# Per-head decays loaded as eight numbers and spread on the chip; zeros of the states on GpSimd

## The chip, the cores and the metric

The kernel runs on one core of a Trainium2 chip. The metric is the device time of one execution in microseconds (us). The time before is the median of three runs; a profiled execution of its own gives the trace that all readings are from. Engines: PE is TensorE, PEld its weight loads, DVE is VectorE, ACT is ScalarE, POOL is GpSimd, SP is SyncE, which issues most of the transfers.

## The reference, cut to what matters

```python
B, H, S, D = 4, 8, 768, 64            # block = 64
rel = pos[:, None] - pos[None, :]
Dmask = where(rel >= 0, lam[:, None, None] ** rel, 0.0)
lam_pow = lam[:, None, None] ** (pos[None, :, None] + 1)
for b in range(S // 64):
    intra = ((qb @ kb.T) * Dmask) @ vb
    inter = (qb * lam_pow) @ kv_state
    out[:, :, sl] = intra + inter
    kv_state = lam ** 64 * kv_state + (kb * lam ** (63 - pos)).T @ vb
x = out, heads side by side            # 3072 x 512
h = x @ w_in                           # 512 x 2048
g = maximum(h, 0) + alpha * minimum(h, 0)
return g @ w_out                       # 2048 x 512
```

`lam` holds one decay for each of the eight heads; all decay factors of the attention are powers of it.

## The kernel before

The attention is computed in blocks of 128 positions, two of them (256 rows) at a time. A unit is one batch entry, one half of the heads (four of them) and 256 rows; `units` lists 24 of them, four to a step `c`. For each unit the raw k, q and v are loaded (`load`, on SP's queue), cast to fp16 (`cast`, k16, q16, v16), k is also multiplied by its decay (`key_decayed`, line 256), q and k are transposed (`transposes`: eight PE transposes at line 284 and a copy of the result `tp` to `qkT`, or a transfer that transposes), and the transposed q is multiplied by its decay (`decayed`, line 299). `cluster(old, new)` then computes the scores `s` of the new unit (line 341), its state update `acc` (line 368), the masked scores `sm` on DVE (line 379, scores times `dmask`), and the output of the old unit (lines 324 and 353), which is copied to `xT`. States are kept in `R`, and in `RD` as blocks with zeros off the diagonal; the zeros are written once at the start (line 120).

`up(c, f)` is the first matrix product of the second part with its activation (lines 431, 439, 448), `down` the second (line 461), `down_last` that of the last step (line 484).

The order of instructions on each engine is the order in which the program issues them: the schedule is manual, each engine's queue is in order, and waits come from the data. The opening is written out by hand (lines 523 to 727), as a list of calls; after it `weave` interleaves attention and matrix products. Transfers go on SP's queue (k, q, v, output), on GpSimd's (the weights, `load_win` and `load_wout`) and two small ones at the start on ScalarE's (lam and alpha). `fill(n)` issues n products of `ident` with itself whose result nobody reads.

All decay tables come from `loglam`, the logarithm of lam on all 128 partitions. Before, `lam` is loaded to all partitions by one transfer whose source has a step of zero over the partitions (line 61), clamped on DVE (`lamc`, line 156), and its logarithm is taken on ScalarE (line 158). An earlier activation of a column of ones (`warm`, line 124) also uses Ln. `loglam` feeds `llp` (lines 192 and 193), the eight logarithmic mask steps of `mask_logs` on DVE (line 173), `key_decay` (line 189, behind a load of the table for Exp), `query_decay` (line 205), `state_decay` (line 197) and `decay_mask` (line 183). The head of the opening is this:

```python
mask_logs(3); mask_logs(0); key_decay()
load(0, 0, "k", 0); cast(0, "k16", "A"); query_decay(2, 1)
...
cast(0, "q16", "G"); decay_mask(3); fill(29)
transposes(0, "V", False); decayed(0, "V"); cast(2, "k16", "A")
...
cast(1, "q16", "G"); cast(0, "v16", "G"); state_decay(); decay_mask(1)
fill(30); cluster(None, 0)
```

"A", "V" and "G" name the engine: ScalarE, VectorE, GpSimd.

Of the kernel before, what the change touches and what calls it, by code (L numbers as in the profile page):

```python
# [11 lines left out]
def kernel(  # L12
# [16 lines left out]
    nc = tc.nc  # L29
    ctx.enter_context(tc.manual_schedule())  # L30
    fp32 = mybir.dt.float32
    fp16 = mybir.dt.float16
    int32 = mybir.dt.int32
    AF = mybir.ActivationFunctionType
    ALU = mybir.AluOpType

    B, H, S, D = q.shape
# [7 lines left out]
    NF = DFF // 128  # L45
    CH = 2 * W

    const = ctx.enter_context(tc.tile_pool(name="const", bufs=1))
# [8 lines left out]
    ps = ctx.enter_context(tc.tile_pool(name="ps", bufs=1, space=bass.MemoryType.PSUM))  # L57
    h_ps_pool = ctx.enter_context(tc.tile_pool(name="hps", bufs=2, space=bass.MemoryType.PSUM))

    lam_sb = const.tile([128, H], fp32, name="lam_sb")  # L60
    nc.scalar.dma_start(
        out=lam_sb,
        in_=bass.AP(tensor=lam.tensor, offset=lam.offset, ap=[[0, 128]] + [list(p) for p in lam.ap]),
    )


    R = {
        (b, hh, n): const.tile([128, 2, D], fp16, name=f"R{b}_{hh}_{n}")
# [4 lines left out]
    RD = {  # L73
        (b, hh): const.tile([128, 2, 2, 2, D], fp16, name=f"RD{b}_{hh}")
        for b in range(B)
        for hh in range(2)
    }
# [35 lines left out]
        x = 4 * (which == "out") + i  # L113
        nc.sync.dma_start(out=gates16[:, x : x + 1], in_=w)

    alpha_sb = const.tile([NF, 128], fp32, name="alpha_sb")
    nc.scalar.dma_start(out=alpha_sb, in_=moe_alpha.rearrange("(t p) -> t p", p=128))

    for t in RD.values():
        nc.vector.memset(t, 0.0)  # L120
    one = const.tile([128, 1], fp32, name="one")
    nc.vector.memset(one, 1.0)
    warm = const.tile([128, 1], fp32, name="warm")
    nc.scalar.activation(warm, one, AF.Ln)
    ident = const.tile([128, 128], fp16, name="ident")
    make_identity(nc, ident)
    ident32 = const.tile([NF, NF], fp32, name="ident32")
    nc.vector.tensor_copy(out=ident32, in_=ident[0:NF, 0:NF])

    rel_i = const.tile([128, 3, 64], int32, name="rel_i")
    for half in range(2):
# [7 lines left out]
        out=drop, in0=rel_i, scalar1=0.0, scalar2=-1e30, op0=ALU.is_lt, op1=ALU.mult  # L141
    )
    rev_i = const.tile([128, 2], int32, name="rev_i")
    for half in range(2):
        nc.gpsimd.iota(
            rev_i[ds(half * 64, 64)], pattern=[[-1, 2]], base=L - 1, channel_multiplier=-2
        )
    rev_f = const.tile([128, 2], fp32, name="rev_f")
    nc.vector.tensor_copy(out=rev_f, in_=rev_i)
    pos_i = const.tile([128, 2, 2, 64], int32, name="pos_i")  # L150
    nc.gpsimd.iota(pos_i, pattern=[[1, 2], [0, 2], [2, 64]], base=1, channel_multiplier=0)
    pos_f = const.tile([128, W], fp32, name="pos_f")
    nc.vector.tensor_copy(out=pos_f, in_=pos_i.rearrange("p e h j -> p (e h j)"))

    lamc = const.tile([128, H], fp32, name="lamc")
    nc.vector.tensor_scalar(out=lamc, in0=lam_sb, scalar1=1e-18, scalar2=None, op0=ALU.max)
    loglam = const.tile([128, H], fp32, name="loglam")
    nc.scalar.activation(loglam, lamc, AF.Ln)
    llv = loglam.rearrange("p (n two) -> p two n", two=2)

    dmask = const.tile([128, 2, NHP, 3, 64], fp32, name="dmask")
# [45 lines left out]
    def slopes():  # L207
# [2 lines left out]
        nc.vector.tensor_scalar(  # L210
            out=oma, in0=at[:, 0:NF], scalar1=-1.0, scalar2=1.0, op0=ALU.mult, op1=ALU.add
        )

    def fill(n):

        t = ps.tile([128, CH], fp32, tag="op", name="op_fill")
        for _ in range(n):
            nc.tensor.matmul(t[:, 0:128], lhsT=ident, rhs=ident, start=True, stop=True)  # L218

    T = {}  # L220
    XT = {}
# [17 lines left out]
    def cast(n, name, eng):  # L239
        t = T.setdefault(n, {})  # L240
        if name == "v16":
            t[name] = half_pool.tile([128, 2, 4, D], fp16, tag=name, name=name)
            copy_on(eng, t[name], raw_of(n)[name])
            return
        if "qk16" not in t:
            t["qk16"] = half_pool.tile([128, 2, 2, 4, D], fp16, tag="qk16", name="qk16")
        copy_on(eng, t["qk16"][:, int(name == "k16")], raw_of(n)[name])
# [21 lines left out]
    def transposes(n, eng, decay=True):  # L269

        t = T[n]
        qkT = qkt_pool.tile([128, 2, 2, 2, L], fp16, tag="qkT", name="qkT")
        if eng == "D":
            nc.sync.dma_start(
                out=qkT.rearrange("p x e h j -> p (x e h) j"),
                in_=t["qk16"].rearrange("p x e h d -> p (x e h d)"),
                transpose=True,
            )
        else:
            tp = ps.tile([128, 2, 2, 2, L], fp16, tag="tk", name="tp")  # L280
            for x in (1, 0):
                for e in range(2):
                    for hp in range(2):
                        nc.tensor.transpose(  # L284
                            tp[:, x, e, hp, :],
                            t["qk16"][:, x, e, ds(2 * hp, 2)].rearrange("p l d -> p (l d)"),
                            ident,
                        )
            copy_on(eng, qkT, tp)
        t["qkT"] = qkT  # L290
        if decay:
            decayed(n)
# [250 lines left out]
    cast(0, "q16", "G")  # L543
    decay_mask(3)
    fill(29)
    transposes(0, "V", False)
    decayed(0, "V")
# [6 lines left out]
    state_decay()  # L554
    decay_mask(1)
    fill(30)
    cluster(None, 0)
    load(0, 1, "k", 1)
# [9 lines left out]
    query_decay(3, 1)  # L568
    key_decayed(2, "V")
    cast(2, "q16", "G")  # L570
    fill(22)
    cluster(0, 1, "A")
    load(1, 0, "k", None)
    load(1, 0, "q", None)
# [6 lines left out]
    cast(2, "v16", "A")  # L581
    decayed(1, "V")
    cast(3, "q16", "A")
    fill(16)
    cluster(1, 2, "A")
    decayed(2, "G")
    transposes(3, "A", False)
    fill(21)
    cluster(2, 3, "A")
    up(0, 3, 0, "h")  # L590
    decayed(3, "G")
# [178 lines left out]
```

## Time and profile before

| | |
|---|---|
| median of 3 runs | 222.5 us (222.31 to 222.65) |
| profiled execution | 222.39 us, span 220.6 us |
| busy, share of the span | PE 94%, DVE 60%, ACT 52%, PEld 51%, POOL 42% |
| chain that ended last, by engine | PE 82%, DMA 5%, ACT 3%, DVE 2%, issue 2% |
| lam's transfer | 4.0 KB, 3.8 us from issue to landing |
| the first twelve loads on SP's queue | 256.0 KB each, the last issued at 9.90 us |

Times in the profile count from the start of the span. In a line of the timeline the first number is the start and the second the time from the first start to the last end, then engine, line, operation, result and operands, shape and count; in brackets stands the idle time in front of it and what ended it. In the chain of waits each piece has its start, its length and what it was. In the table by stage each row gives the busy time of each engine in that stretch, with the number of instructions, the granted PE clock, the share of the DMA engines and the rate of the transfers.

### The profile page before, as it was taken

What the parts mean: (1) busy time and instruction counts of PE and PEld (TensorE: products, weight loads), DVE (VectorE), ACT (ScalarE), POOL (GpSimd) and SP (SyncE); (2) the same over time, 40 slices, a digit from 0 to 9 for tenths busy, and PEclk for the clock granted to TensorE, in tenths of its full rate; (3) what the DMA queues carried; (4) which work ended last, traced back from release to release, by engine and by line L of the source; (5) the groups of instructions that cost most, each with busy time, mean ns of one, the idle gap of its engine ahead of it and who ended that gap; (6) DMA issues with size and microseconds to landing.
All of it is one profiled execution on the core that took longest, in us unless ns stands there. A gap on an engine that the chain in (4) does not pass through costs nothing.

```text
span 220.6 us, 5380 instructions
## 1 busy us (share of the span) xinstructions
PE 208.4 (94%) x2165; PEld 111.7 (51%) x2165; DVE 131.8 (60%) x255; ACT 114.6 (52%) x217; POOL 93.0 (42%) x165
## 2 busy tenths in 40 slices
PE   5697899999996999999999999999999999999994
PEld 5686544564454544545544554544555444444453
DVE  6986488877597974777645656546655544444000
ACT  4897587555464575355465444465544434444121
POOL 3783065533486583676353774433774100000000
PEclk9799999999999999999999999999999999999998
DMA  4999999995999999779448689343231011100212
GB/s 123 296 252 209 273 280 208 199 221 147 151 327 208 299 260 209 153 197 239 117 74 216 149 188 250 83 101 89 51 95 52 0 48 52 48 32 16 95 51 95
DMA packets 62463, 33.92 MB, mean 154 GB/s; under 512 B 18262, under 2 KB 59494, under 8 KB 62438
## 3 DMA queue, kind: packets, MB, share of 16 engines
q1 hardware_dynamic: 58038, 29.37, 53.8%
q0 software_dynamic: 4224, 4.19, 11.5%
q8 instruction: 17, 0.28, 0.6%
q14 instruction: 8, 0.07, 0.1%
q10 hardware_dynamic: 176, 0.01, 0.0%
HBM read 27.28 MB, written 6.29 MB: 152 GB/s over the span
## 4 chain that ended last, share of the span: by engine, by line
PE 82%; DMA 5%; ACT 3%; issue 2%; DVE 2%; SPq 2%; POOL 2%; ACTq 0%; DVEq 0%
PE h_ps L431 35%; PE o_ps L461 30%; PE o_ps L484 6%; PE s L341 4%; PE acc L324 3%; PE acc L353 3%; DMA kraw<-in_k_dram 2%; DMA qkT<-qk 2%; SPq L88 2%; PE acc L368 1%; DVE sm L379 1%; DVE R L403 1%; POOL kdec L256 1%; PE tp L284 1%; ACT RD L399 1%
## 5 line engine op out<-in xcount | busy, mean ns | idle before, releaser
L448 DVE SCALAR_TENSOR_TENSOR g<-m,oma,h_ps 128x512 f16<-128x512 f32 (+1 forms) x98 | 71.2, 736 | 61.3 <-ACT m L439 59.6
L431 PE MATMUL h_ps<-xT,w_in_sb 128*128 128x512 f16 (+1 forms) x392 | 94.7, 375 | 0.1
L439 ACT ACTIVATE m<-h_ps 128x512 f32<-128x512 f32 (+1 forms) x98 | 57.3, 588 | 66.0 <-PE h_ps L431 65.3
L461 PE MATMUL o_ps<-w_out_sb,g 128*128 128x512 f16 x320 | 81.1, 379 | 0.0
L431 PEld LDWEIGHTS <-w_in_sb 128*128 128x128 f16 x392 | 37.6, 98 | 43.5 <-issue 0.2
L461 PEld LDWEIGHTS <-g 128*128 128x128 f16 x320 | 29.8, 98 | 34.0 <-issue 0.2
L379 DVE TENSOR_TENSOR sm<-s,dmask 128x512 f16<-128x512 f32 x48 | 30.8, 683 | 5.7 <-PE s L341 5.1
L299 POOL TENSOR_TENSOR qdT<-qkT,qdecay 128x512 f16<-128x512 f16 (+1 forms) x21 | 22.2, 1058 | 27.0 <-DMA qkT<-qk 11.8
L417 POOL COPY RD<-R 64x128 f16<-64x128 f16 x64 | 18.5, 289 | 34.8 <-DVE R L403 33.1
L474 ACT ACTIVATE o_sb<-o_ps 128x512 f32<-128x512 f32 (+1 forms) x25 | 14.5, 579 | 15.5 <-PE o_ps L484 11.1
L256 POOL TENSOR_TENSOR kdec<-kraw,kdecay 128x512 f16<-128x512 f32 x20 | 21.2, 1061 | 2.2 <-DMA kraw<-in_k_dram 2.1
L226 ACT ACTIVATE xT<-acc 128x512 f16<-128x512 f32 x22 | 13.1, 597 | 14.8 <-PE acc L368 9.8
L403 DVE SCALAR_TENSOR_TENSOR R<-R,rdecay,acc 128x64 f16<-128x64 f16 x64 | 14.2, 274 | 1.8 <-ACT R L400 1.8
L230 POOL CAST v<-vraw 128x512 f16<-128x512 f32 x20 | 13.0, 657 | 2.7 <-DMA vraw<-in_v_dram 2.7
L484 PE MATMUL o_ps<-w_out_sb,g 128*128 128x512 f16 (+1 forms) x80 | 14.0, 336 | 0.0
L218 PE MATMUL op_fill<-ident 128*128 128x128 f16 x140 | 12.0, 258 | 1.4 <-POOL ident masks.py:199 1.4
L341 PE MATMUL s<-qkT 64*64 64x128 f16 x384 | 10.1, 223 | 1.8 <-DMA qkT<-qk 1.7
L324 PE MATMUL acc<-qdT,RD 128*128 128x128 f16 x80 | 8.9, 219 | 3.0 <-DVE R L403 1.8
L218 PEld LDWEIGHTS <-ident 128*128 128x128 f16 x140 | 10.9, 119 | 1.5 <-POOL ident masks.py:199 1.4
L484 PEld LDWEIGHTS <-g 128*128 128x128 f16 x80 | 7.8, 98 | 6.2
L226 ACT ACTIVATE qk<-qraw 128x512 f16<-128x512 f32 x16 | 10.0, 623 | 1.3 <-DMA qraw<-in_q_dram 1.3
L324 PEld LDWEIGHTS <-RD 128*128 128x128 f16 x80 | 5.8, 97 | 9.0 <-ACT qkT L226 1.6
(54 smaller groups left out, 111.4 us busy)
## 6 DMA issues: line engine op xcount, KB each, us to landing
out_dram<-o_sb SPq DMA_DIRECT2D x23, 256.0 KB, 2.5
kraw<-in_k_dram SPq DMA_DIRECT2D x10, 512.0 KB, 5.5
qraw<-in_q_dram SPq DMA_DIRECT2D x10, 512.0 KB, 6.9
vraw<-in_v_dram SPq DMA_DIRECT2D x10, 512.0 KB, 5.8
w_in_sb<-in_moe_w_in_dram POOLq DMA_DIRECT2D x4, 512.0 KB, 8.9
w_out_sb<-in_moe_w_out_dram POOLq DMA_DIRECT2D x4, 512.0 KB, 9.9
kraw<-in_k_dram SPq DMA_DIRECT2D x4, 256.0 KB, 5.4
qraw<-in_q_dram SPq DMA_DIRECT2D x4, 256.0 KB, 5.2
```

Source lines behind the costliest of these rows:

```text
L218: nc.tensor.matmul(t[:, 0:128], lhsT=ident, rhs=ident, start=True, stop=True)
L226: nc.scalar.activation(out, in_, AF.Copy)
L256: engine(eng).tensor_tensor(out=kdec, in0=kr, in1=kdecay[:, ds(4 * hh, 4), :].rearrange("p h e -> p e h").unsqueeze(3).to_broadcast([128, ...
L299: engine(eng).tensor_tensor(out=qdT[:, :, :, p], in0=t["qkT"][:, 0, :, :, p], in1=qdecay[:, hh, :, :, p], op=ALU.mult,)
L324: nc.tensor.matmul(ot[a][:, hp, :].rearrange("p (e j) -> p e j", e=2), lhsT=RD[bb, ho][:, a, hp].rearrange("p h d -> p (h d)"), rhs=to["qd ...
L341: nc.tensor.matmul(s[hl][ds(a * 64, 64), hp, 1 - e, :].rearrange("p (e j) -> p e j", e=2), lhsT=t["qkT"][p, 1, e, hp, ds(a * 64, 64)], rhs ...
L379: nc.vector.tensor_tensor(out=sm, in0=s[hl], in1=mask_of(hl, hh), op=ALU.mult)
L431: nc.tensor.matmul(h_ps[:, 0:n] if bi is None else h_ps[:, 0:n].rearrange("p (e j) -> p e j", e=2), lhsT=w_in_sb[:, gi, ts(f, 128)], rhs=x ...
L439: nc.scalar.activation(m[:, 0:n], h_ps[:, 0:n], AF.Relu, scale=-1.0)
L448: nc.vector.scalar_tensor_tensor(out=g, in0=mv, scalar=oma[:, f : f + 1], in1=hv, op0=ALU.mult, op1=ALU.add)
L461: nc.tensor.matmul(o_ps, lhsT=lhs(c, f, t), rhs=w_out_sb[:, f, :], start=(f == 0), stop=(f == NF - 1),)
L484: nc.tensor.matmul(o_ps[:, 0:n], lhsT=lhs(c, f, t), rhs=w_out_sb[:, f, ts(x, n)], start=(f == 0), stop=(f == NF - 1),)
```

## The change

`lam` is loaded as eight numbers, one on each of eight partitions. DVE clamps them and writes each 128 times (8 x 128), TensorE transposes that to 128 x 8 in PSUM with a corner of the fp32 identity, and Ln reads it from there. The zeros of `RD` are written by GpSimd behind its index patterns instead of by DVE; there they are memsets of 128x512 f16, before they were 128x256 uint32. The column of ones and the activation `warm` are gone. `fill` is defined earlier, eight of its products are issued ahead of the transpose, and three later counts become 23, 17 and 14. alpha's load is issued behind lam's on ScalarE's queue in both kernels. DVE's `lamc` stands ahead of `rev_f` and `pos_f`, and GpSimd's `pos_i` ahead of the zeros.

```diff
--- before.py
+++ after.py
@@ -57,12 +57,11 @@
     ps = ctx.enter_context(tc.tile_pool(name="ps", bufs=1, space=bass.MemoryType.PSUM))
     h_ps_pool = ctx.enter_context(tc.tile_pool(name="hps", bufs=2, space=bass.MemoryType.PSUM))
 
-    lam_sb = const.tile([128, H], fp32, name="lam_sb")
-    nc.scalar.dma_start(
-        out=lam_sb,
-        in_=bass.AP(tensor=lam.tensor, offset=lam.offset, ap=[[0, 128]] + [list(p) for p in lam.ap]),
-    )
-
+    lam_sb = const.tile([H, 1], fp32, name="lam_sb")
+    nc.scalar.dma_start(out=lam_sb, in_=lam.rearrange("(h o) -> h o", o=1))
+
+    alpha_sb = const.tile([NF, 128], fp32, name="alpha_sb")
+    nc.scalar.dma_start(out=alpha_sb, in_=moe_alpha.rearrange("(t p) -> t p", p=128))
 
     R = {
         (b, hh, n): const.tile([128, 2, D], fp16, name=f"R{b}_{hh}_{n}")
@@ -113,19 +112,18 @@
         x = 4 * (which == "out") + i
         nc.sync.dma_start(out=gates16[:, x : x + 1], in_=w)
 
-    alpha_sb = const.tile([NF, 128], fp32, name="alpha_sb")
-    nc.scalar.dma_start(out=alpha_sb, in_=moe_alpha.rearrange("(t p) -> t p", p=128))
-
-    for t in RD.values():
-        nc.vector.memset(t, 0.0)
-    one = const.tile([128, 1], fp32, name="one")
-    nc.vector.memset(one, 1.0)
-    warm = const.tile([128, 1], fp32, name="warm")
-    nc.scalar.activation(warm, one, AF.Ln)
     ident = const.tile([128, 128], fp16, name="ident")
     make_identity(nc, ident)
     ident32 = const.tile([NF, NF], fp32, name="ident32")
     nc.vector.tensor_copy(out=ident32, in_=ident[0:NF, 0:NF])
+
+    def fill(n):
+
+        t = ps.tile([128, CH], fp32, tag="op", name="op_fill")
+        for _ in range(n):
+            nc.tensor.matmul(t[:, 0:128], lhsT=ident, rhs=ident, start=True, stop=True)
+
+    fill(8)
 
 
 
@@ -145,17 +143,23 @@
         nc.gpsimd.iota(
             rev_i[ds(half * 64, 64)], pattern=[[-1, 2]], base=L - 1, channel_multiplier=-2
         )
+    pos_i = const.tile([128, 2, 2, 64], int32, name="pos_i")
+    nc.gpsimd.iota(pos_i, pattern=[[1, 2], [0, 2], [2, 64]], base=1, channel_multiplier=0)
+
+    for t in RD.values():
+        nc.gpsimd.memset(t, 0.0)
+    lamc = const.tile([H, 128], fp32, name="lamc")
+    nc.vector.tensor_scalar(
+        out=lamc, in0=lam_sb.to_broadcast([H, 128]), scalar1=1e-18, scalar2=None, op0=ALU.max
+    )
     rev_f = const.tile([128, 2], fp32, name="rev_f")
     nc.vector.tensor_copy(out=rev_f, in_=rev_i)
-    pos_i = const.tile([128, 2, 2, 64], int32, name="pos_i")
-    nc.gpsimd.iota(pos_i, pattern=[[1, 2], [0, 2], [2, 64]], base=1, channel_multiplier=0)
     pos_f = const.tile([128, W], fp32, name="pos_f")
     nc.vector.tensor_copy(out=pos_f, in_=pos_i.rearrange("p e h j -> p (e h j)"))
-
-    lamc = const.tile([128, H], fp32, name="lamc")
-    nc.vector.tensor_scalar(out=lamc, in0=lam_sb, scalar1=1e-18, scalar2=None, op0=ALU.max)
+    lam_ps = h_ps_pool.tile([128, CH], fp32, tag="h", name="lam_ps")
+    nc.tensor.transpose(lam_ps[:, 0:H], lamc, ident32[0:H, 0:H])
     loglam = const.tile([128, H], fp32, name="loglam")
-    nc.scalar.activation(loglam, lamc, AF.Ln)
+    nc.scalar.activation(loglam, lam_ps[:, 0:H], AF.Ln)
     llv = loglam.rearrange("p (n two) -> p two n", two=2)
 
     dmask = const.tile([128, 2, NHP, 3, 64], fp32, name="dmask")
@@ -210,12 +214,6 @@
         nc.vector.tensor_scalar(
             out=oma, in0=at[:, 0:NF], scalar1=-1.0, scalar2=1.0, op0=ALU.mult, op1=ALU.add
         )
-
-    def fill(n):
-
-        t = ps.tile([128, CH], fp32, tag="op", name="op_fill")
-        for _ in range(n):
-            nc.tensor.matmul(t[:, 0:128], lhsT=ident, rhs=ident, start=True, stop=True)
 
     T = {}
     XT = {}
@@ -568,7 +566,7 @@
     query_decay(3, 1)
     key_decayed(2, "V")
     cast(2, "q16", "G")
-    fill(22)
+    fill(23)
     cluster(0, 1, "A")
     load(1, 0, "k", None)
     load(1, 0, "q", None)
@@ -581,11 +579,11 @@
     cast(2, "v16", "A")
     decayed(1, "V")
     cast(3, "q16", "A")
-    fill(16)
+    fill(17)
     cluster(1, 2, "A")
     decayed(2, "G")
     transposes(3, "A", False)
-    fill(21)
+    fill(14)
     cluster(2, 3, "A")
     up(0, 3, 0, "h")
     decayed(3, "G")
```

## The prediction

> **What bounds the kernel now.** I read the chain of waits first, to see where the change could matter at all. From 25.14 us on the chain is TensorE work nearly without gaps, and the change touches nothing there; so only the start counts, and what it gains or loses is handed on.
>
> ```profile
> 5.47 5.29 DMA kraw<-in_k_dram
> 10.76 0.02 issue
> 10.78 0.63 ACT qk L226
> 11.41 0.09 ACT rdecay L197
> 11.51 0.42 ACT dmask L183
> 11.93 0.02 issue
> 11.96 0.04 DVE sm L379
> ...
> 24.48 0.62 PE op_fill L218 x9
> 25.10 0.04 issue
> 25.14 10.96 PE h_ps L431 x52
> ```
>
> The last early thing that is not engine work is the seventh load, k of `load(0, 1, "k", 0)`, which lands at 10.76. ScalarE's cast, state decay and second pair of masks follow; the first `sm` starts at 11.96. From there to 25.14 small PE, ACT and DVE steps alternate. So the number wanted is when that first `sm` can start.
>
> Next the start by the timeline. lam itself is late:
>
> ```profile
> 4.56 0.17 DVE L156 TENSOR_SCALAR lamc<-lam_sb 128x8 f32<-128x8 f32 x1 [0.82 <-DMA lam_sb<-in_lam_dram]
> 4.76 0.21 ACT L158 ACTIVATE loglam<-lamc 128x8 f32<-128x8 f32 x1 [1.47 <-DVE lamc L156]
> 5.38 3.86 DVE L173 SCALAR_TENSOR_TENSOR dmask<-rel_f,loglam,drop 128x192 f32<-128x192 f32 x8
> 6.43 0.82 POOL L230 CAST qk<-qraw 128x512 f16<-128x512 f32 x1 [3.73 <-DMA qraw<-in_q_dram]
> 7.81 3.36 PE L218 MATMUL op_fill<-ident 128*128 128x128 f16 x30
> ```
>
> Then the table by stage (PE, PEld, DVE, ACT, POOL busy, clock, DMA share, GB/s), for the transfers:
>
> ```profile
> 2.00:3.00 1.00, 1.00 (x12) 1.00 (x11) 0.99 (x5) 0.96 (x1) 0.59 (x3) 1.00 0.20 53
> 3.00:4.00 1.00, 1.00 (x12) 1.00 (x10) 0.74 (x7) 0.20 (x1) 0.00 (x0) 1.00 0.78 169
> 4.00:5.00 1.00, 0.61 (x7) 0.38 (x4) 0.17 (x1) 0.22 (x2) 0.00 (x0) 1.00 1.01 280
> 5.00:6.00 1.00, 0.00 (x0) 0.00 (x0) 0.95 (x4) 1.00 (x1) 0.00 (x0) 1.00 1.14 341
> ```
>
> The loads reach full rate only at 4.4 us. The trace's packets say what runs meanwhile: ACT's queue (lam and alpha, 176 packets) sends its first at 1.78 and its last at 5.05, and lam alone is 128 packets of 32 bytes. While about 7 of these start per 0.1 us, about 30 of the loads' 512-byte packets do; once they are gone, 66.
>
> **The change part by part.**
>
> *lam's transfer.* 128 packets become 8. Before, the first packet starts at 1.78, the first of the 16 engines to finish its eight is counted at 2.74, the last at 4.54. With at most one packet on an engine, I take 2.6; bounds 2.1 (first packet plus the 0.36 us that the quickest engine took from its closing packet to its count) and 4.54 (nothing gained).
>
> *lam's path.* Before: DVE 0.17, then Ln. After: DVE 0.17 over 8x128, a fp32 transpose on TensorE, Ln out of PSUM. The nearest row is the transpose of alpha, 0.23; with 0.1 for each handover, Ln starts near 3.2, 1.5 us earlier than 4.76 (bounds: 0.4 later if lam still lands at 4.54; 1.9 earlier). `warm` is gone, but Ln's table load stands ahead of Ln in ACT's order without a wait, as it did at 1.68, and ends at 2.96: it costs nothing as long as Ln starts after that, 1.28 if it moved behind the wait.
>
> *The loads.* Against the 290 GB/s of later, microseconds 2 to 5 lack (237+121+10)/290 = 1.27 us of transfer. Bounds for what returns: 0 (a slow start whatever ACT's queue does) and 1.27. I take 1.1, since alpha's packets stay. The seventh load then lands at 9.65, and the load and weight queues behind it shift too.
>
> *The zeros.* DVE loses 2.19 us that lay before lam arrived: worth nothing by itself. GpSimd gets eight memsets behind `pos_i`, which ends at 2.71; they are 128x512 f16, where DVE had 128x256 uint32. Queued behind them is the cast of q (6.43, ready when its load lands), which half of the first transposes needs. Rows: memset 128x1 0.10, 128x128 0.20, so 0.10 + 0.83 ns x 511 = 0.52 for 512. Bounds per memset: 0.43 (the beginnings overlap, as those of 128x1 do) and 0.70 (0.52 times 0.82/0.61, the ratio of a cast beside DVE's mask work to one alone). I take 0.50: zeros end at 6.7, the cast at 7.5 instead of 7.25. Lower end 7.0, upper 9.1.
>
> The Trainium skill (SBUF — State Buffer, "Who interferes with whom") speaks against the upper end: a DVE instruction with two SBUF inputs contends with a GpSimd instruction that reads SBUF, not with one that only writes it. The slower cast, a reader, agrees; no run here shows a GpSimd memset beside the masks. By the rule the cast would end at 7.7 at most.
>
> *DVE.* Its eight mask steps start 1.5 earlier and end at 7.7; key decay and the copy of the first transposes follow, 10.18 to 10.86 before, near 8.7 to 9.4 after; the query decay ends near 9.9 instead of 11.38.
>
> *ScalarE.* All up to the first two masks (end 9.91) comes 1.5 earlier; then it waits for the seventh load at 9.65, and cast, decay and mask end at 10.8 instead of 11.93.
>
> *TensorE.* New: fill(8) (0.95 us from 1.37, at 107 ns each), then the transpose, which waits for lam. Behind that wait stand fill(29) and everything else. fill(29) starts near 3.1 and takes at most 3.1 us, so it ends by 6.2, before the second half of the transposes (7.5 to 7.8); if lam landed at 4.54 it would end near 8.1 and be the last. Then fill(30) runs ahead of the first `cluster`. Its speed is the open point: before, the clock granted was 0.50 from 7.84 to 11.26, after a stretch of 3.4 us with PE busy 0.64; at full clock a fill takes 56 ns (22 in 1.39). At 56 ns it ends near 9.5, at 107 near 11.0.
>
> ```profile
> 1.03:4.42 3.39, 3.05 (x29) 1.00 0.40 92
> 4.44:7.83 3.39, 0.64 (x11) 1.00 1.14 312
> 14.68:18.07 3.39, 2.42 (x63) 1.00 1.23 204
> 21.51:24.90 3.39, 2.49 (x64) 1.00 1.20 229
> ```
>
> (PE busy, clock, DMA share, GB/s in four 3.4 us stretches.) After stretches with 2.4 to 2.5 busy, and in them, the clock stayed at 1.00; after 0.64 it halved. The fills show that the first stretch's 1.00 is only the absence of a record: they ran at 107 ns until 4.43. In the changed kernel the stretch 4.43 to 7.84 holds the rest of fill(29) (1.0 at 56 ns, 1.8 at 107), 0.5 of transposes, and the start of fill(30): 1.7 to 2.5 busy. I take full clock.
>
> The Trainium skill (TensorE: Matmul & The Clock Gate, "What's actually happening") says that half clock is the default, that a busy window of about 3.4 us releases it, and that the window runs freely and doesn't start with the kernel. The first half agrees with the rows; that the window's phase could differ is shown by no run here, and by it the halving could fall elsewhere.
>
> *Fill counts.* 22 to 23 and 16 to 17 add 0.06 each in gaps of 0.29 (13.48 to 13.77) and 1.0; 21 to 14 takes 0.39 off ahead of a wait that ends at 20.61 by ACT and DVE. Nothing; without those gaps 0.06 each. alpha's load keeps its place on ACT's queue.
>
> *The sum.* The first `sm` needs the mask (10.8), the scores (fill end 9.5, copy 9.4, plus 0.45: 10.0) and DVE (9.9). It starts near 10.85 instead of 11.96: 1.1 us earlier. v and the key decay on GpSimd, done at 10.73 before, come near 10.4, as does the issue of the weights; they are needed at 21.6 at the earliest, and the first chunk lands at 18.12. From 25 to 60 PE has some 0.4 us of gaps, so the shift is kept. 222.39 (profiled execution: span 220.6 and 1.8 around it) minus 1.1 is 221.3; that execution lies 0.1 under the median of 222.5, so 221.4.
>
> **The rivals.**
>
> *Half clock.* fill(30) runs from 7.8 to 11.0, scores 11.45, `sm` 11.5: 0.45 earlier, and nothing if the q cast is later by as much: 222.0 to 222.5. For: 1.7 us busy lies between the 0.64 that halved the clock and the 2.4 that kept it. Against: the upper estimate.
>
> *The loads don't move.* The seventh still lands at 10.76 and ScalarE still ends at 11.93: 222.4. For: the first load's packets begin at 2.3, which a slow start explains as well. Against: their rate doubles just when ACT's packets end.
>
> *GpSimd is the bound (slower).* At 0.70 per memset the q cast ends at 9.1, transposes at 9.4, fill(30) at 12.6 on half clock, `sm` at 13.1: 1.15 later, 223.6; at 0.60, 222.9. The point is a cast ending at 7.65 with half clock (0.52 per memset), or 9.1 with full clock. For: 512 elements each instead of 256, on an engine whose cast ran a third slower here. Against: the memset rows.
>
> That the change doesn't do what it says is excluded by the instruction order: eight memsets on GpSimd, one transpose, 8x1 loaded.
>
> **How the numbers follow.** What can be told from no change here is about 0.2%, 0.44 us. Forecast 0.56, all faster. Half clock 0.18: 0.10 faster, 0.06 same, 0.02 slower. Loads unmoved 0.09: 0.08 same, 0.01 slower. GpSimd 0.17: 0.01 same, 0.16 slower. Together 0.66, 0.15, 0.19. The forecast's own range is 220.8 (loads 1.27 earlier, and 0.3 from the steps behind) to 222.0. Including half clock, unmoved loads and the GpSimd case up to 0.60 gives 220.8 to 222.9.
>
> **What would show it.** Right: lam's DVE step near 2.7 and Ln near 3.2; over 150 GB/s in microsecond 2 to 3; the cast of k at L226 near 9.7 instead of 10.78; PE clock 1.00 through 8 to 11; the first `sm` near 10.85 and the long run of `h_ps` near 24.0 instead of 25.14. Wrong: a GpSimd cast after 8, a clock of 0.50 under fill(30), or GB/s as before; and a long run that starts early while the span doesn't follow.

## The result and the profile after

The changed kernel is slower: 224.75 us (median of six, 223.41 to 225.08) against 222.62 for the kernel before in the same comparison (median of six, 222.31 to 223.19), a ratio of 1.0086 with a 95% interval of 1.0057 to 1.0115. Its profiled execution took 224.54 us with a span of 222.8, against 222.39 and 220.6: 2.15 more.

The timeline of the changed kernel shows the loss in its first seven microseconds:

```profile
2.30 4.20 DVE L152 TENSOR_SCALAR lamc<-lam_sb 8x128 f32<-8x128 f32 x1
2.43 4.08 DVE L156 CAST rev_f<-rev_i 128x2 f32<-128x2 int32 x1
2.64 3.79 POOL L150 MEMSET RD<- 128x512 f16 x8
2.73 3.91 DVE L158 CAST pos_f<-pos_i 128x256 f32<-128x256 int32 x1
...
6.56 0.27 PE L160 MATMUL lam_ps<-ident,lamc 8*128 8x8 f32 x1 [4.15 <-DVE rev_f L156]
6.87 0.18 ACT L162 ACTIVATE loglam<-lam_ps 128x8 f32<-128x8 f32 x1 [3.85 <-PE lam_ps L160]
...
12.97 2.03 DVE L297 TENSOR_TENSOR qdT<-qkT,qdecay 128x256 f16<-128x256 f16 x1
13.66 1.05 POOL L254 TENSOR_TENSOR kdec<-kraw,kdecay 128x512 f16<-128x512 f32 x1
...
72.58 0.42 PE L339 MATMUL s<-qkT 64*64 64x128 f16 x16 [1.00 <-DMA qkT<-qk]
```

lam was there in time: DVE began the clamp at 2.30. But the clamp of 8x128 numbers took 4.20 us. It began beside GpSimd's index pattern `pos_i` (2.33 to 2.70), which the eight memsets follow without a gap, and all three DVE steps begun there ended at 6.50 to 6.64, when the memsets did (2.64 plus 3.79 is 6.43). TensorE stood 4.15 us waiting, and Ln started at 6.87 instead of 4.76, later by 2.11.

In the chain of waits the standstill is the first large piece, and what waited behind it follows:

```profile
2.38 4.12 DVE lamc L152
...
6.56 0.27 PE lam_ps L160
6.83 3.21 PE op_fill L124 x29
...
14.93 1.28 DVE sm L377 x2
...
25.36 1.16 issue
...
28.04 0.27 PE h_ps L429
```

The ledger against the kernel before: Ln +2.11; first `sm` 14.93 instead of 11.96, +2.97; long run of `h_ps` 28.04 instead of 25.14, +2.90. Later 0.73 comes back: TensorE's idle time from the start of the long run to its last product is 1.46 instead of 2.19, almost all of it one wait for a transposing transfer of q and k. It is the last line of the timeline above, 1.00; in the timeline of the kernel before it was:

```profile
70.43 0.42 PE L341 MATMUL s<-qkT 64*64 64x128 f16 x16 [1.74 <-DMA qkT<-qk]
```

2.90 minus 0.73 is 2.17; the span grew by 2.2.

Between Ln and the first `sm` another 0.9 was lost on balance. `qdT`, with two SBUF inputs, took 2.03 beside GpSimd's cast and its product `kdec`, which read SBUF; before it took 0.42. The scores were ready at 13.45 and the masks at 12.91, so this step was last. At 0.42 it would have ended at 13.39, and `sm` could have begun near 13.5: by this estimate from the rows `qdT` cost about 1.4 of the 2.97, and Ln's 2.11 only about 1.5, since waits that stood in the kernel before (DVE's 0.57 for the masks, ScalarE's 0.87 for the seventh load) took up the rest. This share wasn't tested by itself, and the second experiment below lost as much without a long `qdT`.

The table by stage shows that the loads did move (columns as in the prediction):

```profile
2.00:3.00 1.00, 0.41 (x4) 0.14 (x2) 1.00 (x5) 1.00 (x1) 0.88 (x4) 1.00 0.80 218
3.00:4.00 1.00, 0.00 (x0) 0.00 (x0) 1.00 (x3) 0.01 (x1) 1.00 (x3) 1.00 1.09 324
4.00:5.00 1.00, 0.00 (x0) 0.00 (x0) 1.00 (x3) 0.00 (x0) 1.00 (x4) 1.00 0.80 209
5.00:6.00 1.00, 0.00 (x0) 0.00 (x0) 1.00 (x3) 0.00 (x0) 1.00 (x4) 1.00 0.87 233
```

218 GB/s instead of 53 in microsecond 2 to 3, and the first load landed at 3.78 instead of 5.45. But the rates of 4 to 6 fell to 209 and 233 where the kernel before had 280 and 341, and of the 1.7 us only 0.66 was left at the fourth load (7.48 instead of 8.14).

### The profile page after: what moved, and what is told of

It is laid out like the page before. It is cut to its first block, busy times and chain, and to the rows that moved or that the text cites. A ratio compares the mean times of both kernels' runs of the same rounds, so it can differ in the third digit from the quotient of the medians.

```text
span 222.8 us, 5388 instructions
## 1 busy us (share of the span) xinstructions
PE 208.5 (94%) x2169; PEld 111.9 (50%) x2169; DVE 133.4 (60%) x246; ACT 114.2 (51%) x216; POOL 95.5 (43%) x173
## 4 chain that ended last, share of the span: by engine, by line
PE 82%; POOL 4%; DVE 4%; DMA 4%; issue 3%; ACT 2%; POOLq 0%; SPq 0%; DVEq 0%; ACTq 0%
PE h_ps L429 34%; PE o_ps L459 28%; PE o_ps L482 6%; DMA qkT<-qk 4%; PE s L339 3%; PE op_fill L124 3%; PE acc L322 2%; PE acc L351 2%; DVE lamc L152 2%; POOL kdec L254 2%; POOL qdT L297 2%; PE acc L366 1%; PE tp L282 1%; ACT RD L397 1%; DVE R L401 1%
## 5 line engine op out<-in xcount | busy, mean ns | idle before, releaser
L228 POOL CAST v<-vraw 128x512 f16<-128x512 f32 x20 | 12.2, 616 | 2.6 <-DMA vraw<-in_v_dram 2.6
```

## The experiments

Theory P: DVE's one-input steps between SBUF operands stand still as long as GpSimd's memsets run, and that is the loss. Rival S: the clamp of 8x128 with a repeated operand is slow by itself. Rival T: TensorE's path (the wait for the transpose, cold products) is the loss. Later ones: D, the landing of the seventh load sets the opening once P is gone; F against G, a pause of TensorE near 25 us belongs to a place in its instructions (F) or to the time and place in the schedule (G). All ratios are to the kernel before, on the same chip; its median was 222.61 to 222.76 on the three chips used. In the expectations E1, E3, E4, E5 and E10 are the runs whose labels begin so.

**1. Zeros back on DVE, all else as changed** (`e1_zeros_on_dve`). The zeros stand again ahead of the identity.

```diff
+    for t in RD.values():
+        nc.vector.memset(t, 0.0)
     ident = const.tile([128, 128], fp16, name="ident")
...
-    for t in RD.values():
-        nc.gpsimd.memset(t, 0.0)
```

> The changed kernel with the zeros back on DVE, ahead of the identity as in the kernel before; all else as changed. Theory P (in the changed kernel DVE's lamc, rev_f and pos_f stand still while GpSimd's eight memsets run, 2.64 to 6.43, and all three end at 6.5 to 6.64 for that reason): lamc takes under 0.3 us and ends near 4.0 (DVE's own zeros end at 3.05, three steps follow), Ln starts near 4.4 instead of 6.87, the first sm near 11.4, and the time is 221.5 to 222.6. Rival S (lamc itself is slow, since it reads one number 128 times on eight partitions, or lam's data come late): lamc still takes 4 us and ends near 7.9, the time is above 225. Rival T (the PE wait and the cold clock behind it cost the time, whatever DVE does): lamc is short but the first sm stays after 13 and the time near 224.5.

221.81 us (220.74 to 223.16), ratio 0.9951 (0.9918 to 0.9985). Its timeline:

```profile
3.31 0.21 DVE L152 TENSOR_SCALAR lamc<-lam_sb 8x128 f32<-8x128 f32 x1
3.88 0.18 ACT L162 ACTIVATE loglam<-lam_ps 128x8 f32<-128x8 f32 x1 [0.86 <-PE lam_ps L160]
10.19 0.63 ACT L224 ACTIVATE qk<-kraw 128x512 f16<-128x512 f32 x1 [0.93 <-DMA kraw<-in_k_dram]
```

The same clamp takes 0.21 instead of 4.20, and the loss is gone: P holds, S and T fall. The first `sm` starts at 11.36. The last line is the seventh load's cast: it waited 0.93 for the transfer and began 0.59 earlier than before, not 1.1. Rates of 209 and 225 GB/s in microseconds 4 to 6 show the same dip as in the changed kernel.

**2. The kernel before, with its zeros alone moved to GpSimd, behind `pos_i`** (`e2_before_zeros_pool`).

```diff
-    for t in RD.values():
-        nc.vector.memset(t, 0.0)
...
+    for t in RD.values():
+        nc.gpsimd.memset(t, 0.0)
```

> The kernel before with one part of the change alone: the zeros on GpSimd behind pos_i. lam is still loaded to all partitions and goes through no transpose. Theory P: rev_f and pos_f, which stand ahead of lamc on DVE here, end only with the memsets near 6.5, lamc follows near 6.6 instead of 4.56, Ln near 6.85, and the time is 224 to 225, as in the changed kernel. Rival S: lamc stays at 4.56 and the time at 222.5. Rival T (PE wait): no transpose here, so time at 222.5.

224.94 us (224.08 to 226.87), ratio 1.0101 (1.0063 to 1.0139): the zeros alone make a loss as large, with no transpose in the kernel. Its timeline:

```profile
2.30 4.15 DVE L147 CAST rev_f<-rev_i 128x2 f32<-128x2 int32 x1
6.42 0.63 POOL L230 CAST qk<-qraw 128x512 f16<-128x512 f32 x1
6.50 0.57 DVE L156 TENSOR_SCALAR lamc<-lam_sb 128x8 f32<-128x8 f32 x1
```

Now the cast of two columns stands still, and the clamp behind it is held again, by GpSimd's cast of q, to 7.07. From there the way differs: `qdT` took 0.42, but the clock was 0.50 from 8.30 to 15.13, under fill(30) and the scores, and the first `sm` began at 14.61 all the same. So the collision of `qdT` is no necessary part of the loss. Nor is the halved clock: six of the ten executions had a mean granted clock of 0.997 or more, and they took 224.08 to 225.73. Rates at 4 to 6 were 293 and 339, without the dip: it comes with the new lam load, not with the zeros.

**3. The clamp with two inputs** (`e3_lamc_two_inputs`): the larger of lam and itself instead of lam and a constant, which equals the clamp for every lam above 1e-18.

```diff
-    nc.vector.tensor_scalar(
-        out=lamc, in0=lam_sb.to_broadcast([H, 128]), scalar1=1e-18, scalar2=None, op0=ALU.max
+    nc.vector.tensor_tensor(
+        out=lamc, in0=lam_sb.to_broadcast([H, 128]), in1=lam_sb.to_broadcast([H, 128]), op=ALU.max
```

> The changed kernel with lamc as the maximum of lam with itself (two inputs) instead of with a constant; the clamp falls away, which changes nothing for decays near 1. Theory P, in the form that only DVE's one-input steps between two tensors in SBUF stand still: lamc ends by 2.8, the transpose runs at 2.8, Ln starts near 3.1; rev_f and pos_f still end near 6.5, and so llp still comes near 6.6 and the masks start near 7; the time falls by 0 to 1 us against the changed kernel, to 223.7 to 224.7. Theory P in the form that everything on DVE stands still: no difference, lamc still ends at 6.5. Rival S: lamc still takes 4 us.

224.11 us (223.42 to 224.81), ratio 1.0051 (1.0014 to 1.0089). Its timeline:

```profile
2.31 0.27 DVE L152 TENSOR_TENSOR lamc<-lam_sb 8x128 f32<-8x128 f32 x1
2.50 3.95 DVE L156 CAST rev_f<-rev_i 128x2 f32<-128x2 int32 x1
6.51 0.56 DVE L196 COPY llp<-loglam 64x4 f32<-64x4 f32 x1
```

A two-input step in the same place runs through in 0.27, and Ln starts at 3.02. The next one-input step stands still instead, and what stands behind it in DVE's order with it: masks at 7.28. The first `sm` came at 14.43, after a `qdT` of 1.30 beside GpSimd's `kdec`. So it is the kind of step that is held, not what it computes.

This two-input step ended at 2.58, before the first memset began; it ran beside `pos_i`, beside which the one-input clamp takes 0.47 where no memset follows (first line below, from the fifth experiment). A step of two SBUF inputs beside memsets themselves stands in the trace of the fourth experiment, and it was not held: `qdT` took 0.41 there.

```profile
2.30 0.47 DVE L152 TENSOR_SCALAR lamc<-lam_sb 8x128 f32<-8x128 f32 x1
...
16.24 1.94 POOL L581 MEMSET RD<- 128x512 f16 x4
16.80 0.41 DVE L298 TENSOR_TENSOR qdT<-qkT,qdecay 128x256 f16<-128x256 f16 x1
```

The Trainium skill (SBUF — State Buffer, "Who interferes with whom") says this: a DVE copy, cast or tensor_scalar in a mode that uses both ports shares a port pair with GpSimd, whoever issues first keeps it for its whole instruction, and the other "fully blocks". These runs agree that the step is held, 4.20 against 0.21, but it was held through eight GpSimd instructions in a row and not through one; which mode a step is in, the profile doesn't show. The prediction weighed only the rule next to it, on steps with two inputs, and that one agrees too: `qdT` took 0.41 beside memsets, and 2.03 beside a cast and a product that read SBUF.

**4. Half of the memsets at the start, half behind the last opening cast** (`e5_four_early_four_late`).

```diff
-    for t in RD.values():
-        nc.gpsimd.memset(t, 0.0)
+    for (b, hh), t in RD.items():
+        if b < 2:
+            nc.gpsimd.memset(t, 0.0)
...
     cast(3, "v16", "G"); load_win(3)
+    for (b, hh), t in RD.items():
+        if b >= 2:
+            nc.gpsimd.memset(t, 0.0)
```

> The changed kernel with four of GpSimd's memsets (batch entries 0 and 1) where the eight were, and the other four much later, behind the cast of v of unit 3 and the last weights of the first matrix. Theory P: the four end near 4.55, lamc, rev_f and pos_f end right behind at 4.6 to 4.7, Ln starts near 5.0, 1.9 us earlier than in the changed kernel, and the time is 222.3 to 223.2. Rival S: lamc still ends near 6.5 and the time is as changed, 224.7. Rival T: Ln comes earlier and the time hardly moves.

221.98 us (221.10 to 223.31), ratio 0.9951 (0.9917 to 0.9984). Its timeline:

```profile
2.30 2.33 DVE L153 TENSOR_SCALAR lamc<-lam_sb 8x128 f32<-8x128 f32 x1
2.64 1.92 POOL L151 MEMSET RD<- 128x512 f16 x4
```

Half the memsets, half the standstill: DVE's step ends with the fourth memset, not between two of them. Ln starts at 5.00, 1.12 later than in the first experiment, but the first `sm` only 0.30 later: ScalarE's wait for the seventh load shrank from 0.93 to 0.39 and took up part of it. That fits a time below what was expected.

**5. Zeros split, none beside DVE's early steps** (`e4_zeros_split`): batch entry 0 on DVE ahead of `ident32`, entry 1 on DVE behind `pos_f`, 2 and 3 on GpSimd late, as in the fourth.

```diff
+    for hh in range(2):
+        nc.vector.memset(RD[0, hh], 0.0)
     ident32 = const.tile([NF, NF], fp32, name="ident32")
...
+    for hh in range(2):
+        nc.vector.memset(RD[1, hh], 0.0)
...
+    for (b, hh), t in RD.items():
+        if b >= 2:
+            nc.gpsimd.memset(t, 0.0)
```

> The changed kernel with the zeros taken out of lam's way on both engines: those of batch entry 0 on DVE ahead of the fp32 identity, those of entry 1 on DVE behind pos_f, those of entries 2 and 3 on GpSimd behind the cast of v of unit 3. Theory P: lamc ends near 2.6, Ln starts near 3.1 (E1: 3.88), the masks start near 3.7 (E1: 4.47). Under the theory that the seventh load binds the opening, as its cast waited 0.93 us in E1, the first sm stays near 11.36 and the time at 221.2 to 222.2, as in E1. Rival (lam's path binds it): sm near 10.6 and the time 0.7 us under E1's.

221.36 us (median of eight, 220.83 to 221.91), ratio 0.9936 (0.9914 to 0.9959): clearly below both kernels. Its timeline:

```profile
10.09 0.63 ACT L226 ACTIVATE qk<-kraw 128x512 f16<-128x512 f32 x1 [0.98 <-DMA kraw<-in_k_dram]
```

lam's path is as short as forecast (Ln at 3.14, masks from 3.80), yet the first `sm` starts at 11.26, 0.10 before that of the first experiment: the seventh load binds (theory D).

**6. The load of k ahead of the load of v** (`e10_split_k_before_v`): the fifth, with `load(0, 1, "k", 0)` issued ahead of `load(0, 0, "v", 1)`.

```diff
+    load(0, 1, "k", 0)
     load(0, 0, "v", 1)
     mask_logs(1)
-    load(0, 1, "k", 0)
```

> E4 with the seventh load (k of unit 2) issued ahead of the sixth (v of unit 1). Theory D (with lam and the zeros out of the way, the landing of that k sets the first sm): it lands 0.9 us earlier, its cast starts near 9.2 instead of 10.09, the first sm near 10.4 instead of 11.26, and the long run of products may start up to 0.8 us earlier, as far as the pause in fill(13) and later loads let it; time 220.6 to 221.4. Rival (another wait stands right behind): the cast starts earlier and the first sm does not follow.

221.20 us (median of twelve, 220.71 to 223.05), ratio 0.9932 (0.9904 to 0.9961), not to be told from the fifth. The cast came at 9.73 without waiting and the first `sm` at 10.90, 0.36 earlier, not the 0.86 expected: ScalarE's cast of the fourth load, which stands ahead, came at 7.92 instead of 7.36. But the long run began at 25.23 (fifth: 25.04): TensorE waited 1.71 for `qdT` of a later unit, until 17.31 (fifth: 1.17, for a cast of v, until 17.12). D holds for the first `sm`; whether it holds for the end this profile can't say, since the profiled execution was the longest of the twelve, 223.05.

**7. The pause of TensorE.** In the chain after stands "issue" 1.16 at 25.36, between nine and four products of fill(13). It lies behind nine products in the first, fifth and sixth experiments too. Four runs move it by changing fill counts ahead of it: seven more products (`e8_e1_seven_fills_more`, fill(14) to 21 in the first experiment), four fewer (`e6_e1_four_fills_fewer`, fill(17) to 13 in the first; `e7_split_four_fills_fewer`, the same in the fifth; `e9_split_fill8_to_4`, the first fill(8) to 4 in the fifth).

```diff
# e8
     transposes(3, "A", False)
-    fill(14)
+    fill(21)
# e6 and e7
     cast(3, "q16", "A")
-    fill(17)
+    fill(13)
# e9
-    fill(8)
+    fill(4)
```

> E1 with fill(14) back at fill(21), so TensorE's program is 14 instructions longer ahead of fill(13). Theory F: the pause moves to behind the second product of fill(13), eleven products (0.6 us) follow it, the state products at line 322 start near 24.1 and the time rises by 0.2 to 0.5 us against E1. Rival G: the pause stays after nine products, and the time is E1's.

> E1 with fill(17) made fill(13), so TensorE's program is 8 instructions shorter ahead of fill(13) in front of the last early cluster. In the changed kernel, E1, E3 and E5 PE stands still for 1.0 to 1.2 us inside that fill(13), after nine of its products, waiting for nothing that the profile shows; in the kernel before the same instruction number falls behind the fill, where PE waits for R anyway. Theory F (the pause belongs to an instruction number, the fetch of the next piece of the program): the pause moves behind the thirteenth product, the state products at line 322 start near 23.4 instead of 23.78, and the time falls by 0.2 to 0.5 us against E1. Rival G (the pause belongs to that place or to a time): it stays after nine products and the time is E1's.

> The zeros split as in the run beside it and fill(17) made fill(13). Theories P and F together: the fastest of these, 220.9 to 221.8; if neither adds anything to E1, 221.8.

> E4 with the first fill(8) made fill(4): TensorE's program is again 8 instructions shorter ahead of the last early cluster, but the products are taken from the stretch before lam arrives and not from the middle of the opening. Theory F: the pause falls behind the thirteenth product of fill(13), where PE waits for R, and the state products at line 322 of E1 (here 324) start near 23.2 to 23.5 instead of 23.75; the time falls by 0.2 to 0.5 us against E4, 220.9 to 221.3, and the clock is granted as in E4. If the pause didn't matter: E4's time.

The timeline of the kernel with seven more:

```profile
21.38 0.27 PE L126 MATMUL op_fill<-ident 128*128 128x128 f16 x2
22.98 0.79 PE L126 MATMUL op_fill<-ident 128*128 128x128 f16 x11 [1.33 <-issue]
```

Seven more ahead, and it comes seven products sooner, behind two. Four fewer, and no pause shows inside the fill: by F it lies behind all 13, where TensorE waits for `R` anyway. In the changed kernel and the first experiment it stands behind the same nine products at 25.36 and at 22.17, so it isn't tied to a time. F fits all of these and G doesn't: the place is an instruction's number. An instruction transfer of 16 KB lies close by each time (in the first experiment 20.96 to 21.90, the pause from 22.17; in `e8` 20.76 to 21.70, the pause from 21.65); that it is the cause is a guess from this alone.

The times don't follow, and the three misses are these: 222.89 us for `e6` (ratio 0.9989, 0.9956 to 1.0021), 222.14 for `e7` (0.9948, 0.9913 to 0.9983), 222.29 for `e9` (0.9979, 0.9949 to 1.0009). `e8` has 222.11 (0.9968, 0.9944 to 0.9993), inside what was expected, but not for the reason given: its state products start at 23.61 and its long run at 24.89, as in the first experiment (23.62 and 24.91). In the profile of `e6` the long run began 0.53 earlier than in the first experiment, but then the wait for the transposing transfer near 70 us was 2.02 (0.84 there), and the clock was 0.50 from 70.03 to 73.45; in that of `e7` it was 0.50 from 15.06 to 21.89. The times of `e6` go with its clock: six of its twelve executions had a mean granted clock of 0.998 or more and took 221.03 to 222.57, the other six 0.990 to 0.992 and 223.21 to 224.56; in the first experiment none of ten lay below 0.997. Whether the missing fills let the clock drop isn't shown: that of `e7` dropped 0.15 after its shortened fill began (14.91), that of `e6` more than 50 us later.

**8. The load order and the shorter first fill together** (`e11_both`): the sixth experiment with the edit of `e9`.

```diff
-    fill(8)
+    fill(4)
```

> E10 with fill(8) made fill(4) as well. Theories D and F together: 220.3 to 221.2, the fastest; if neither adds anything: E4's time, 221.4.

222.01 us (221.31 to 223.55), ratio 0.9964 (0.9935 to 0.9994). The first `sm` came at 10.44 and the long run at 24.90, both earlier than in the fifth, but the clock was 0.50 from 18.00 to 21.41 and the wait near 70 us 1.77. An earlier opening is taken back there. What sets that wait (0.78 to 2.02 in these profiles) stays open.

## Why the prediction was wrong

The step that failed is the term "DVE 0.17" in *lam's path*: it measured 4.20, and Ln started at 6.87 instead of the 3.2 forecast. The prediction costed what the memsets do to GpSimd's queue, and weighed what DVE's masks do to the memsets, but never what the memsets do to DVE's steps of one input that stand beside them: `lamc`, `rev_f` and `pos_f`. Its sentence "DVE loses 2.19 us that lay before lam arrived: worth nothing by itself" was where the price came in: those zeros now occupied GpSimd just when lam, much earlier, arrived. A second term went with it: `qdT` was carried over at its old length, 0.42, and took 2.03 once the shift put it beside GpSimd's reading steps.

Point by point:

- *lam's transfer*, 2.6 forecast: the last of eight was counted at 2.06. Right in kind, even earlier.
- *The zeros*, 0.50 each: 3.79 for eight is 0.47. q's cast ended at 7.11 (forecast 7.5). So the rival that GpSimd is the bound had the right sign for a wrong reason: q's cast was not late. By that rival's own steps the casts that leave no gain would end near 7.95 (half clock) and 9.45 (full), not 7.65 and 9.1; nothing else hangs on these two.
- *The loads*, 1.1: the seventh's cast came 0.59 (first experiment) to 0.69 (fifth) earlier. Right in kind, mis-sized: the missing 1.27 us of transfer time were taken to return nearly whole, but the rate fell at 4 to 6 us. What causes the dip stays open; it is in every profile with the new lam load and not in the second experiment.
- *TensorE*, full clock: in the changed kernel it stood idle from 2.41 to 6.56, and the first clock record begins at 11.89. Ahead of that 29 fills took 3.27 us, 113 ns each, so the table's 1.00 at 8 to 11 is only the absence of a record; fill(30) took 2.42. The forecast's case arose in the first experiment, and there it holds: the record of 1.00 begins at 6.83, and fill(30) took 1.84, 61 ns each.
- "From 25 to 60 PE has some 0.4 us of gaps, so the shift is kept": the view ended too early, and "TensorE work nearly without gaps" from 25.14 on was misread with it. The wait at 68 to 72 (1.74 before) lies beyond 60 and took 0.73 off the loss; in the other direction it takes gains back.

Without those terms the sum's total comes out: the first experiment is the change without the memsets on GpSimd, and its profiled execution took 221.25 us where the sum gave 221.3 (median 221.81, forecast 221.4). But its parts don't: the first `sm` was 0.60 earlier, not 1.1, and the long run 0.23 earlier, not 1.1, while the wait near 70 us was 0.84 instead of 1.74: 0.23 and 0.90 make the 1.1. So this agreement is mostly luck.

## What to carry to other kernels

Work that is moved to GpSimd because it is "off the path" must be read against what DVE does in the same microseconds: a run of cheap memsets held a step of 0.2 us for 4 us. Put such work late, or where DVE has only steps like `qdT` in the fourth experiment (two inputs, 0.41 beside memsets), and check by the ends: DVE steps of different sizes that all end together with a GpSimd instruction were held. And follow a gain at the start past every wait for a transfer to the end before it is counted.

## What the runs showed of the hardware

- Eight memsets in a row held DVE for all eight, 2.30 to 6.50, and four for four, to 4.63; the waiting step never got in between two. Even a cast of 128x2 (0.15 alone) and a copy of 64x4 (0.56 instead of 0.16, beside GpSimd's cast of q) were held.
- With lam's load of 128 packets of 32 bytes beside it, the first 256 KB load landed at 5.45 us, in the second experiment too; with eight packets it landed at 3.78.
- The clock's records come in steps of 3.41 us, and the first lies at 6.83 in the first experiment and at 8.59 in `e6`, which differs by four fills only. This agrees with the rule of the Trainium skill that the prediction named (TensorE: Matmul & The Clock Gate, "What's actually happening"): the window doesn't start with the kernel. So whether a gap in TensorE's work halves the clock can differ between executions, as the two groups of `e6` suggest, and one profile can't settle it.
